# mLSTM and mixture-of-experts kernel: another searched order of work

## The chip, the cores and the metric

The kernel runs on one core of a Trainium2 chip. The metric is device time in microseconds; the kernel before takes 465.71 us as the median of three runs (465.06 to 465.93).

## The reference

An mLSTM attention layer over 4 sequences, 8 heads, 768 steps and head size 40, and behind it a feed-forward layer on all 3072 tokens, everything in float32:

```python
for t in range(S):
    m_new = np.maximum(f_gate[:, :, t] + m, i_gate[:, :, t])
    f_stab = np.exp(f_gate[:, :, t] + m - m_new)
    i_stab = np.exp(i_gate[:, :, t] - m_new)
    m = m_new
    C = f_stab[:, :, None, None] * C + i_stab[:, :, None, None] * np.einsum('bhd,bhe->bhde', vt, kt)
    n = f_stab[:, :, None] * n + i_stab[:, :, None] * kt
    h_tilde = np.einsum('bhde,bhe->bhd', C, qt)
    nq = np.einsum('bhd,bhd->bh', n, qt)[:, :, None]
    denom = np.maximum(np.abs(nq), 1.0)
    y[:, :, t] = o * h_tilde / denom
...
h = x @ w_in
relu6 = np.clip(h + 3.0, 0.0, 6.0)
g = h * relu6 / 6.0
return (g @ w_out).astype(np.float32)
```

Here vt, kt, qt are step t of v, k and q, o is the sigmoid of o_gate, and w_in and w_out (320 x 2048 and back) come as float64.

## The kernel before, in words

The recurrence is computed in chunks of 128 steps. A pair is one chunk of one sequence; there are 24 pairs, each in two groups of four heads ("quads"), which makes 48 chunk tasks. The tokens of the pairs are gathered into seven blocks, numbered 0 to 6, of 2, 2, 4, 4, 4, 4 and 4 pairs. A block first has its attention computed, then it is transposed (xa, line 613), split into a high and a low part for exact float32 products (xh on ACT, line 621, and xl on DVE, line 623), multiplied with w_in in 16 slices (mm1, line 738), passed through the activation (re on ACT, line 755, and gg on DVE, line 757), split again (gh, line 205 or 207, and gl, line 768), and multiplied with w_out in 8 steps per pair (mm2, lines 784 to 786). Block 0 has its second product in native float32 (line 781). Each pair's accumulator is copied out (ev) and stored.

The attention of a chunk task has loads (st, line 354, and nat, line 359), a weighing of the keys by the gates (vp, line 368 on ACT, line 370 on DVE or POOL), small matmuls in groups (xya and xyb, lines 479 to 512: S and K of a task, and B of the task before), the state C (line 452 or 455, its first form a copy on line 205 or 207), a gate window gw (a mask gm on line 401, a shift gc on line 406, an exponential gx on line 416, or on line 414 in four pieces with the shift in it), the products with it (fr, line 419), and the outputs (b1, b2, r1 to r3, o1 and o2, lines 464, 469 and 593 to 598). Four gate blocks (g0 to g3) are made by scans on DVE (lines 274 to 286); a transposition on PE (pT) and three copies (cTs, cT, gTs) lead to wT, the weights of vp.

The weights arrive as float64 in sixteen slices of 640 KB, eight of w_in (raw buffers called rawi) and eight of w_out (rawo). Three raw buffers are shared by all of them. Float64 is taken apart by hand: ACT reads a slice three times (w1, line 648; w2, line 653; w3, line 658), DVE puts it together (w4 to w6, lines 663, 664 and 669 or 674), and a slice of w_in is then split into whi, wlo and the two tail pieces th and ts (lines 205, 207, 692, 693 and 695), a slice of w_out later into vh and vl (lines 205 or 207, and 710).

Nothing of this is ordered by a loop at run time or by a scheduler. A table of 1,886 entries, the string ORDER, fixes it. Each entry is a number of an operation, a letter for the engine (p is PE, d is DVE, a is ACT, g is POOL, q is the SP queue, n means that it is left out because another operation has taken it in) and, behind it, the numbers of the buffers that it takes. Entries of the form F are filler matmuls (line 232), whose result nobody reads. The kernel walks through the table once and emits each operation on its engine's queue; each engine executes its queue in order, and waits where its inputs aren't there or its buffer isn't free. The part that does this:

```python
        for tok in ORDER.split():
            if tok[0] == "F":
                fill(int(tok[1:] or 1))
                continue
...
            i = next(k for k, ch in enumerate(tok) if ch.isalpha())
            key, engs, fn, after, get = T.ops[int(tok[:i])]
            e, slots = tok[i], tok[i + 1 :].split("/") if len(tok) > i + 1 else []
...
            fn(e)
            done.add(key)
```

The table itself was searched outside of the kernel.

Of the kernel before, what the change touches and what calls it, by code (L numbers as in the profile page):

```python
# [57 lines left out]
719p0 F 132q 145g F 767d0 133g 134n 146n 122n 123d 768d 120d 721p10 80q0 949a F 950d F F F 81a 948a 770d 951g F 113d1 114d 769d 135a 952q1 F 124d 771g
125d 772d1 773d 774d 777p0 775d 953a1 956d 776d 780p10 957d 783g 784p20 954a0 955a 157q1 778a0 779d 147a 958d 129q4 130d F F 996q2 781a 782d 997a0 F F
785a 786d 128q4 722p0 960a 158q 159g 939d 137d 138n 139d 160g 998a1 963q0 1000d 143q0 965a0 144d 136d 907n 1068p0 1071p1 1069a 1070d 1074p0 22q 23d  # L60
964a2 1001d 142q1 723p0 959a 1072a 967d 1073d 155q1 156g 1077p1 25d 968d 1003q1 999a 1002d 1117p0 966a 969d 1075a 1076d 1004a0 1078a 1080p0 26d 1007d
149d 150n 962g 1079d 1083p1 151d 148d 27d 961d 971a 1005a1 970a 973g 1116p0 1081a 1082d 1086p0 1084a 1085d 140d0 141d 972d 1006a 198q3 154q0 168q3
1010q2 1011a1 1014d 1008d 197q2 169q2 170g 724p0 152d 1087a 1088d 163d 161a 1089p1 1092p0 24g 29d 1012a0 1013a 1009d 1118p 162d 153d 1090a 1091d 171g
172g 787d2 985q0 986a2 31p31 164n 165d 725p0 1093a 1094d 989d 32d 36p 182q4 28q 974q1 987a1 988a 35a 33a 975a0 1015d 1016d 990d 991d 1095p0 976a0
1017q2 978d 993d 979d 34a 1018a1 1021d 37d 1096a 1097d 166d1 1120p 1022d 167d 977a 980d 38a 1119p 1098p1 1101p0 1019a1 1020a 1023d 1121p 173a 1099a
239q0 183q4 174d 39a 184g 191n 175d 1122p 176n 177d 788d 789d 1100d 981a 984g 726p0 982a 983d 185q2 1102a 1103d 1024q0 1025a1 1028d 992a 1104p1 1107p0
1029d 995g 178d 179d 792d0 1026a0 1027a 793d 126q0 1030d 1123p 1125p 127a 994d 1108a 1109d 1038q1 1110p0 1031q2 252q0 1033a1 30d 790d 240q 224q1 795d
1032a0 1035d 1036d 1105a 1034a 1111a 1040a0 791g 1106d 1112d 1124p 1037d 1052a 1113p1 1114a 797p0 798a1 794d 796d 1115d 803a 799d 186q 200g 201n 187d
1039a1 1127p 1053g 804p1 217g 40q 192d 193g 805a 806d 800p0 801a 226g 1126p 188n 802d 189a 190d 230n 194d 1045q0 1046a2 1136p1 1141p0 1137a0 199d
727p0 211q2 1138d 1146p1 223q1 1042d 1049d 1043d 1041a 1142a1 1143d 1044d 213d 1050d 1151p0 225d 1128p 1047a1 1048a 1051d 214n 1129p 1144a0 1145d  # L70
210q0 180q0 202a 241d 195d0 203d 1147a1 1148d 204g 205d 196d 251q3 41q 280g 1139a1 236q4 212g 1054d 1140g 253a 1130p 1132a0 242n 206n 207d 1152a0 42d
44d 43g 1153d 1131p 1134a1 237q4 1149a2 1150d 728p0 218d 1055d 1154a3 1155g 219n 220d 227n 228a 284n 308q3 281n 1156p1 1161p0 1216p0 1218p 1157a1
1158d 45d 46d 267d 208d 209d 1217p0 47q 215a 1162a0 1056a 1163d 1166p1 1171p0 49d 1159a0 1219p 1160g 1164d1 1165d 216d 729p0 282a 1057d 1167a1 1172a0
1168d 1176p1 1169d2 1170g 1173d 1181p0 231d 232n 1174d3 181a 1177a1 295q1 1220p 221d 222d 229d 1178d 271g 238g 245g 233d 730p0 246d 234d 235d 807d1
1058a 254g 51p31 247n 248d 277q2 243a 346q0 1175g 1059g 1060a 1061g 244d 296q 278q2 1182a0 297d 1183d 1062d 808d 809d 255g 1063g 52a 1222p 54a 53a 55a
279a 1221p 1179a0 1184a1 731p0 249d1 56p 265q1 266a 58a 57d 59a 268n 1180g 258n 259d 260n 1186p0 264q1 261d 256a 257d 250d 298n 1185d 50d 301g 1064a
1191p1 1192a1 1193d 1223p 732p0 1065d 262d 263d 1194a2 1195g 310g 355g 272d 1196p1 1224p 269a 270d 340n 273n 274d 733p0 1225p 1197a0 1198d 810d 1133q
1201p1 811g 1199a3 1200g 1187a1 285d 1188d 1206p0 292q4 293q4 275d 375q0 311n 312a 276d 283d 309a 286n 287d 294g 734p0 1202a0 1189d0 299a 1203d 1204d1
1190d 1205d 817p1 288d 1207a1 1208d 302d 289d 1066a 307q3 349q2 350q 323d 1226p 1228p 362q1 812d2 818a0 819d 813d 1211p0 1212a0 815d 814d 816d 823a
1067g 1227p 1209a0 1229p 333q1 374q2 334q2 1210g 824p1 1213d 1214a2 1215g 303n 304d 300d 735p0 305d0 313d 825a 826d 820p0 821a 822d 327n 324n 336d  # L80
306d 337n 1230p 314g 315d 316n 1232a2 364d 1231p 1234d0 1236p1 1241p0 1237a1 1238d 1239d1 321q4 322g 1246p1 1242a0 365d 1243d 1251p0 320q4 1244d3 317d
736p0 1240d 1252a1 1245d 1316p0 1247a0 1253d 318d 319d 376a 325a 328d 329g 335g 351g 352d 353a 1319p0 1317p0 1318p0 330d 1248d 394n 326d 1254a0 1255g
1256p0 1257a1 366a 1258d 338a 737p0 341d 342g 331d 1249d2 347q3 1261p1 1266p0 348d 343d 1250d 1323p 1320p 1322p 1259a1 1260d 332d 1267a0 418q4 1268d
390d 339d 738p0 354d 356d 357g 361q3 344d 345d 1271p0 1321p 1269a3 1262a1 1263d 1276p1 1270d 363d 358d 739p0 359d1 1264a0 1265g 1277a0 1327p 1272a1
1325p 1326p 1278d 1281p1 367d 1273d 1274a2 360d 1286p0 1324p 391d 392a 290q0 291a 1275g 1282a1 1283d 1330p 381g 1291p1 1284d0 1285d 368g 369d 370n
371d 740p0 478n 1287a1 1329p 1331p 388q2 389d 403q3 404a 827d0 1288d 48q 405q0 406q 407g 408n 1279a1 411g 372d 377d 382d 383n 1280d 1292a0 1334p 1293d
830d 384d 387q4 828d 61q 60q 62d 373d 829d 1233q 1296p0 1328p 1335p 378d 379a 63g 1294a2 1295d 1297a0 1332p 1289a3 1290g 1301p1 420g 1302a1 1333p
1298d 1299a0 380d 741p0 395d 1303d 393d 385d 1306p0 396n 386d 424g 1300g 1337p 1307a0 409a 397d 459q1 402q1 471q0 831g 1308d 431q1 432a 742p0 837p1
838a1 1304d1 417q3 1339p 1305g 1311p0 1312a1 412d 413n 398d 399d 832d1 833d 834d 835d 836g 1338p 1342p 1336p 1313d 1314a2 410d 414d 839d 840p0 1135q
460q 843g 487g 504g 419g 743p0 425d 426n 415d0 841a 842d 844p1 845a 400q0 1341p 1343p 846d 1356p0 1361p1 1309d3 1310g 1315d 1345p 491g 1357a0 1340p  # L90
1346p 64d 65d 66d 421d 416d 1347p 1358d 1359d0 68q 427d 1366p0 1352a2 1350d1 1360d 1344p 401a 1362a1 1363d 1371p1 1364d1 422a 423d 1365d 1367a0 1368d
69d 1369d2 1376p0 461d 1372a1 1373d 1370d 485q0 465g 446g 1381p1 447g 1351q 457q2 456q2 444q3 67q 1235q 445a 1437p0 430q4 744p0 569q2 472q4 437g 438d
1354d1 1374a3 1348a0 1438p0 433g 1436p0 1439p0 1353q 570q 607q1 434n 435a 436d 1375d 439n 440d 1442p 1377a0 1378d 458a 428d 429d 1440p 448a 462n
# [828 lines left out]
```

## Time and profile before

| | |
|---|---|
| median of 3 runs | 465.71 us (465.06 to 465.93) |
| the profiled execution | 464.87 us |
| its span, first to last instruction | 463.2 us |
| granted TensorE clock, mean | 0.996 |
| PE busy | 449.1 us (97%) |
| DVE busy | 298.8 us (65%) |
| ACT busy | 215.8 us (47%) |
| POOL busy | 122.4 us (26%) |
| chain that ended last | PE 85%, DVE 9%, ACT 2%, issue 1%, DMA 1% |

The busy shares are means over the whole span. They differ by stage, so the stages are read one by one from the windows. A matmul's duration includes its way through the array, and consecutive ones overlap; the distance of two starts is what one adds.

### The profile page before, as it was taken

The page shows a single profiled execution, that of the slowest core. Times are in us where ns is not written, and L with a number is a line of the kernel's source. Part 1 is how long each engine was busy: PE and PEld are TensorE (multiplying, and loading weights), DVE is VectorE, ACT ScalarE, POOL GpSimd, SP SyncE. Part 2 cuts the span into 40 slices and gives each one's busy share as a digit, 9 for nine tenths or more (in the row PEclk, how much of TensorE's full clock was granted, in tenths as well). Part 3 has the DMA queues.
Part 4 walks back from the last instruction along what each step waited for, and adds up shares of the span by engine and source line. Part 5 has one row for each costly group of instructions (what it writes and reads, how often), then busy time and mean ns, then how long its engine had stood idle before and what let it go on. Part 6 is the DMA issues. An engine that isn't in the chain of part 4 may idle for free.

```text
span 463.2 us, 12600 instructions
## 1 busy us (share of the span) xinstructions
PE 449.1 (97%) x5243; PEld 388.3 (84%) x5249; DVE 298.8 (65%) x752; ACT 215.8 (47%) x482; POOL 122.4 (26%) x155
## 2 busy tenths in 40 slices
PE   8879989999999999999999999999999999999997
PEld 4547767899888888988889988988989898989896
DVE  6999999978866376856655763576555646443423
ACT  5788798777343434263343353243551232321231
POOL 3152225265311307502213134132112201020130
PEclk9989999999999999999999999999999999999999
DMA  6998887276304450244421442432322000010001
GB/s 208 281 315 265 234 258 203 59 176 169 94 20 119 119 151 4 78 142 121 115 77 44 131 139 60 108 102 89 101 69 78 1 1 1 16 57 1 1 1 57
DMA packets 24977, 49.38 MB, mean 107 GB/s; under 512 B 2840, under 2 KB 15960, under 8 KB 24920
## 3 DMA queue, kind: packets, MB, share of 16 engines
q1 hardware_dynamic: 24696, 47.89, 35.5%
...
q10 hardware_dynamic: 224, 0.69, 0.5%
...
## 4 chain that ended last, share of the span: by engine, by line
PE 85%; DVE 9%; ACT 2%; issue 1%; DMA 1%; SPq 0%; DVEq 0%; ACTq 0%
PE h L738 35%; PE acc L784 11%; PE acc L785 11%; PE acc L786 11%; PE xya L506 3%; PE xya L479 3%; PE pw L232 2%; PE xya L489 2%; PE xa L613 2%; PE xya L512 2%; PE acc L781 1%; DVE on L597 1%; DMA st<-in_qk_dram 1%; DVE on L598 1%; DVE gv L757 1%
## 5 line engine op out<-in xcount | busy, mean ns | idle before, releaser
L755 ACT ACTIVATE g<-h,half 128x512 f32<-128x512 f32 (+1 forms) x96 | 61.8, 651 | 128.3 <-PE h L738 92.9
L784 PE MATMUL acc<-vh,gh 128*128 128x320 f32 x352 | 111.5, 317 | 0.0
L757 DVE SCALAR_TENSOR_TENSOR g<-g,h 128x512 f32<-128x512 f32 (+1 forms) x96 | 61.2, 640 | 77.4 <-ACT g L755 77.3
L785 PE MATMUL acc<-vl,gh 128*128 128x320 f32 x352 | 108.6, 309 | 0.0
L786 PE MATMUL acc<-vh,gl 128*128 128x320 f32 x352 | 108.5, 308 | 0.0
L768 POOL TENSOR_TENSOR gl<-g,gh 128x512 fp32r<-128x512 f32 (+1 forms) x40 | 48.7, 1222 | 183.6 <-DVE gh L207 104.2
L738 PE MATMUL h<-xh,whi 128*128 128x512 f32 (+1 forms) x224 | 83.9, 375 | 2.4 <-DVE gv L757 1.7
L738 PE MATMUL h<-xh,wlo 128*128 128x512 f32 (+1 forms) x224 | 80.8, 361 | 0.0
L738 PE MATMUL h<-xl,whi 128*128 128x512 f32 (+1 forms) x224 | 80.5, 360 | 0.0
L784 PEld LDWEIGHTS acc<-vh,gh 128*128 128x128 f32 x352 | 66.0, 188 | 2.5
L785 PEld LDWEIGHTS acc<-vl,gh 128*128 128x128 f32 x352 | 66.1, 188 | 1.8
L786 PEld LDWEIGHTS acc<-vh,gl 128*128 128x128 f32 x352 | 66.0, 188 | 0.0
L738 PEld LDWEIGHTS h<-xh,whi 128*128 128x128 f32 x224 | 42.0, 187 | 11.4 <-DVE gv L757 3.7
L205 ACT CAST gh<-g 128x512 fp32r<-128x512 f32 (+1 forms) x53 | 30.0, 571 | 39.8 <-PE acc L785 19.5
L738 PEld LDWEIGHTS h<-xh,wlo 128*128 128x128 f32 x224 | 42.1, 188 | 6.9
L768 DVE TENSOR_TENSOR gl<-g,gh 128x512 fp32r<-128x512 f32 (+1 forms) x56 | 40.0, 722 | 12.2 <-ACT gh L205 10.9
L738 PEld LDWEIGHTS h<-xl,whi 128*128 128x128 f32 x224 | 42.1, 188 | 4.5
L738 PE MATMUL h<-xl,wtl 128*128 128x512 f32 (+1 forms) x112 | 40.5, 361 | 0.0
L738 PE MATMUL h<-xh,wtl 128*128 128x512 f32 (+1 forms) x112 | 40.2, 359 | 0.0
L419 DVE TENSOR_TENSOR gw<-xya,gw 128x256 f32<-128x256 f32 x48 | 20.0, 416 | 10.7 <-PE xya L489 7.4
L452 DVE SCALAR_TENSOR_TENSOR C<-C,dec,xya 128x42 f32<-128x42 f32 x100 | 20.6, 251 | 9.1 <-PE xya L489 9.0
L207 DVE CAST gh<-g 128x512 fp32r<-128x512 f32 (+1 forms) x43 | 19.3, 451 | 7.5 <-PE acc L785 6.1
(136 smaller groups left out, 683.2 us busy)
## 6 DMA issues: line engine op xcount, KB each, us to landing
...
rawo<-in_w_out_dram SPq DMA_DIRECT2D x8, 640.0 KB, 7.9
...
rawi<-in_w_in_dram SPq DMA_DIRECT2D x7, 640.0 KB, 8.5
...
on<-in_on_dram SPq DMA_DIRECT2D x5, 640.0 KB, 4.9
rawi<-in_w_in_dram ACTq DMA_DIRECT2D x1, 640.0 KB, 4.2
```

The source lines that it names most:

```text
L205: nc.scalar.copy(dst, src)
L207: E(c).tensor_copy(dst, src)
L419: add(f"fr{nm}", "d", lambda e: nc.vector.tensor_tensor(V["gw", task][:, cp], V["xy", "S", nm][:, :, 0:128].rearrange("p c (j t) -> p j c ...
L452: nc.vector.scalar_tensor_tensor(Cn[:, j], cur[:, j], dc[:, j : j + 1], kv[:, hc, j], ALU.mult, ALU.add)
L479: nc.tensor.matmul(xy[h * Q : h * Q + Q, c, j * Q : j * Q + Q], st[rs, j, h], st[rs, j, 2 + (h != c)], start=True, stop=True)
L738: nc.tensor.matmul(hp[:, :n], w, x[:, :n], start=k == 0, stop=k == len(seq) - 1)
L755: nc.scalar.activation(V["g", nm], V["h", nm][:, :n], AF.Relu, bias=half, scale=1.0 / 6.0)
L757: add(f"gg{nm}", "d", lambda e: nc.vector.scalar_tensor_tensor(V["g", nm], V["g", nm], 1.0, V["h", nm][:, :n], ALU.min, ALU.mult), [f"re{n ...
L768: add(f"gl{nm}", "gd", lambda e: E(e).tensor_sub(V["gl", nm], V["g", nm], V["gh", nm].bitcast(F32)), [f"gh{nm}"], kind="tt", n=n, lock=1)
L784: nc.tensor.matmul(acc, gh[:, ts_], V["VH", f // 4][:, f % 4, :], start=f == 0, stop=False)
L785: nc.tensor.matmul(acc, gh[:, ts_], V["VL", p][:, f % 2, :], start=False, stop=False)
L786: nc.tensor.matmul(acc, gl[:, ts_], V["VH", f // 4][:, f % 4, :], start=False, stop=f == NF - 1)
```

## The change

Only the table ORDER is another. The operations, their code and their dependences stay. It came out of the same search with another measure: the end of an order is judged as its mean over draws of random delays on loads and operations, in place of its end without delays. The new table has 1,883 entries, 46 F for 49. It also gives some operations to other engines: DVE has 658 entries for 685, ACT 369 for 365, POOL 163 for 143. Every line of the table differs; the first of them:

```diff
--- before.py
+++ after.py
@@ -51,78 +51,78 @@
 ORDER = """
-1a 908a0 T F F F F 2q 3d 4d 5d F F F F F 6d 7d 9d F 909a0 912d 913d F F 910a0 107p0/0 F 0q 16d 11p0 12d 919q1 911a 914d 916d 917d 14a F F 920a1 923d
...
+1a 908a0 T F F F 2q 3d F F 0q 16d 5d 6d F F F F 4d 7d 910a0 9d 85p0/0 11p0 F F 96p10 F F 909a0 911a 86a 919q1 920a1 941q2 921a1 922a 82q0 912d 913d
...
```

Three places show how it moves instructions. The first is ACT from its third pass over weight slice 0 on. In the names a number follows each buffer; rawi_128 is slice 0, the next ones in both lists are slice 1, cTs and wT are the gate weights, gw the gate window. Before, cTs stands directly behind slice 0:

```order
7 L658 ACTIVATE lwi_155<-rawi_128,tiny 128x640
8 L205 COPY cTs<-pc_169 128x32
9 L648 ACTIVATE yi_188<-rawi_177 128x640
10 L653 ACTIVATE lwi_191<-rawi_177 128x640
11 L388 ACTIVATE gw_0_194<-gb_0_0_195 128x256
12 L319 ACTIVATE dec<-pc_169 128x32
13 L321 ACTIVATE wT<-wT 128x32
```

And with the change (rawi_226 is slice 2, rawi_188 slice 3):

```order
7 L658 ACTIVATE lwi_149<-rawi_128,tiny 128x640
8 L388 ACTIVATE gw_0_152<-gb_0_0_153 128x256
9 L648 ACTIVATE yi_186<-rawi_184 128x640
10 L653 ACTIVATE lwi_190<-rawi_184 128x640
11 L658 ACTIVATE lwi_190<-rawi_184,tiny 128x640
12 L653 ACTIVATE lwi_228<-rawi_188 128x640
13 L306 ACTIVATE eG<-pc_161 128x32
14 L648 ACTIVATE yi_232<-rawi_226 128x640
15 L648 ACTIVATE yi_235<-rawi_188 128x640
16 L205 COPY cTs<-pc_161 128x32
```

The copy cTs has moved behind all of slice 1 and the first reads of slices 2 and 3.

The second place is the SP queue, which issues the loads, from its first weight slice on; st and nat are the data of chunk tasks, gsc a small scratch store that waits for the first gate scan. Before:

```order
3 L640 DMA rawi_177<-in_w_in_dram 128x1280
4 L285 DMA gsc<-f_s 4x8x128
5 L359 DMA nat_0_1_216<-in_nat_dram 128x412
6 L354 DMA st_0_0_218<-in_qk_dram 112x640
7 L359 DMA nat_0_0_220<-in_nat_dram 128x412
```

With the change:

```order
3 L640 DMA rawi_184<-in_w_in_dram 128x1280
4 L640 DMA rawi_188<-in_w_in_dram 128x1280
5 L354 DMA st_0_0_193<-in_qk_dram 112x640
6 L285 DMA gsc<-f_s 4x8x128
7 L640 DMA rawi_226<-in_w_in_dram 128x1280
8 L359 DMA nat_1_1_244<-in_nat_dram 128x412
9 L359 DMA nat_0_0_247<-in_nat_dram 128x412
```

Slice 3 is now issued right behind slice 1, and slice 2, whose buffer was slice 0's, ahead of the chunk loads.

The third place is PE around the first mm1 matmul of block 0 (h_0). Before, it follows the group xya4 (here xya_559, with S and K of one task):

```order
155 L479 MATMUL xya_559<-st_0_0_557 64x64 x8
156 L489 MATMUL xya_559<-nat_0_0_542 64x42 x8
157 L738 MATMUL h_0_610<-xh_533,whi 128x256
158 L738 MATMUL h_0_610<-xl_534,whi 128x256
```

With the change, the group xya5 (here xya_614) ends directly ahead of it, while xya4 stands ahead of the transposes:

```order
155 L506 MATMUL xya_614<-C_0_0_0_588,st_0_0_557 64x42 x4
156 L512 MATMUL xya_614<-nat_0_0_533,gw_0_345 64x42 x8
157 L479 MATMUL xya_614<-st_0_1_388 64x64 x8
158 L489 MATMUL xya_614<-nat_0_1_531 64x42 x8
159 L738 MATMUL h_0_677<-xh_598,whi 128x256
```

One group more precedes the first mm1.

## Rows read from the trace of the kernel before

**Rows 1.** Windows: length, then busy us of PE, PEld, DVE, ACT, POOL; clock, DMA.

```profile
0.00:34.62 34.62, 29.00 (x385) 16.67 (x392) 28.31 (x83) 24.39 (x53) 12.00 (x23) 0.95 0.86 268
34.62:76.34 41.72, 37.98 (x443) 30.08 (x435) 39.90 (x101) 34.86 (x66) 13.74 (x16) 1.00 0.82 241
...
sum 463.20, PE 449.12 PEld 388.31 DVE 298.84 ACT 215.75 POOL 122.44; mean PE 149.71 PEld 129.44 DVE 99.61 ACT 71.92 POOL 40.81
```

**Rows 2.** Groups of instructions by form: busy us, mean ns, idle before and releaser.

```profile
L232 PE MATMUL pw<-ones 128*128 128x512 bf16 x43 | 14.9, 475 | 3.1 <-issue 1.8 <-DVE tiny L179 1.3
```

**Rows 3.** The window from ACT's first weight slice to its third xh.

```profile
5.59:33.13 27.54, 23.18 (x343) 14.47 (x348) 23.69 (x67) 21.44 (x48) 7.44 (x10) 0.96 0.92 281
```

**Rows 4.** PE's waits from 76.34 on: for whom, us, times, longest.

```profile
PE xa L613 <- ACT on L205: 0.8, 1, 0.8
PE xa L613 <- DVE g L757: 0.6, 1, 0.6
```

**Rows 5.** ACT's groups by form, from 5.59 to 33.13.

```profile
L658 ACT ACTIVATE lwi<-rawi,tiny 128x640 f16<-128x640 f32 x5 | 5.0, 998 | 0.0
L653 ACT ACTIVATE lwi<-rawi 128x640 uint16<-128x640 uint32 x5 | 4.5, 909 | 0.0
L648 ACT ACTIVATE yi<-rawi 128x640 f32<-128x640 f32 x5 | 4.0, 792 | 2.1 <-DMA rawi<-in_w_in_dram 2.1
...
L388 ACT ACTIVATE gw<-gb 128x256 f32<-128x256 f32 x4 | 1.5, 382 | 0.8 <-PE gb L384 0.8
L205 ACT CAST whi<-yi 128x512 fp32r<-128x512 f32 x2 | 1.2, 595 | 0.0
...
L205 ACT COPY C<-xya 128x84 f32<-128x84 f32 x2 | 0.5, 229 | 2.3 <-DVE gw L419 2.2
```

**Rows 6.** ACT's groups by form, whole span.

```profile
L414 ACT ACTIVATE gw<-gw,cT 128x64 f32<-128x64 f32 x88 | 23.3, 338 | 0.0
...
L368 ACT ACTIVATE nat<-nat,wT 128x40 f32<-128x40 f32 x60 | 14.7, 318 | 11.1 <-DMA nat<-in_nat_dram 11.1
```

**Rows 7.** Timeline of ACT, its third pass over slice 0: start, us.

```profile
7.05 1.00 ACT L658 ACTIVATE lwi<-rawi,tiny 128x640 f16<-128x640 f32 x1
```

**Rows 8.** Loads of w_in slices: the one from ACT's queue, then SP's seven.

```profile
rawi<-in_w_in_dram ACTq DMA_DIRECT2D x1, 640.0 KB, 4.2
...
DMA to landing us min/median/max: 6.5/8.5/10.6
```

**Rows 9.** Timeline of PE: the first matmuls of the first two mm1.

```profile
34.62 0.38 PE L738 MATMUL h<-xh,whi 128*128 128x256 f32 x1
...
35.67 0.28 PE L738 MATMUL h<-xh,whi 128*128 128x256 f32 x1
```

**Rows 10.** Timeline of PE: one xya group to the next, a native second product.

```profile
114.46 0.44 PE L506 MATMUL xya<-C,st 40*64 40x42 f32 x16
...
115.54 0.66 PE L613 MATMUL xa<-ident,on 128*128 128x128 f32 x4
...
75.48 1.24 PE L781 MATMUL acc<-vr,gv 128*128 128x320 f32 x4
```

**Rows 11.** DVE's groups by form, whole span.

```profile
L674 DVE CUSTOM_DVE_ANT_0 yi<-yi,lwi 128x1280 uint16<-128x1280 uint16 x8 | 6.7, 843 | 0.3
...
L692 DVE TENSOR_TENSOR wtl<-yi,wtl 64x128 fp32r<-64x128 f32 x8 | 3.4, 425 | 0.3
...
L693 DVE TENSOR_TENSOR wtl<-yi,wtl 64x128 fp32r<-64x128 f32 x8 | 2.3, 288 | 0.2
```

**Rows 12.** Timeline of DVE: a sum of gate block 1.

```profile
38.28 0.99 DVE L276 TENSOR_TENSOR f_s<-f_s,m_s 64x128 f32<-64x128 f32 x1
```

**Rows 13.** Timeline of POOL and DVE near 117 us, and of DVE near 75.

```profile
116.61 1.57 POOL L710 TENSOR_TENSOR vl<-vr,vh 128x640 fp32r<-128x640 f32 x1 [2.77 <-ACT vh L205]
...
116.68 1.78 DVE L401 TENSOR_TENSOR gw<-gw,mask 128x256 f32<-128x256 f32 x1
...
75.07 0.41 DVE L401 TENSOR_TENSOR gw<-gw,mask 128x256 f32<-128x256 f32 x1
```

More of the change, by code (lines that the diff above doesn't have):

```diff
@@ L58 @@
[L58 to L93, printed above, removed]
@@ new lines @@
+721p0 109d 768d 110a 111n 112d 719p10 955a 958d 81a F F F F 770d 113d1 143q1 146n 129q2 130a 134g 144g F 965a1 147a 769d F 157q0 28q 124d 125d 772d1
+128q0 722p0 771g 777p0 114d 773d 774d 135a 959a 775d 776d 783g 137a F F 960a 780p10 F 781a0 778a 784p20 136d F 1002d F F 138n 139d 723p0 962g 779d
+785a 786d 782d 966a 974q1 975a1 976a0 967d 968d 969d 185q1 154q2 155q0 907n 1068p0 149d 1069a 1070d 158q 169q3 159g 140d0 978d 971a 972g 1071p1 1072a
+1074p0 1073d 1077p1 150n 151d 148d 141d 156a 724p0 197q1 961d 970a 1075a 1076d 1078a 1079d 1080p0 1083p1 160g 29d 977a 985q0 986a2 1003q2 1005a1
@@ new lines @@
+1257a1 333q4 330d 737p0 331d 332d 337n 1319p0 340n 341d 342n 343d 338a 1262a0 1263d 339d 1234a0 1317p0 1322p 1264a0 1266p0 1323p 1258d 1271p1 1259a1
+362q1 361q3 347q3 348g 738p0 354d 1321p 363g 1265g 1267a0 1268d 1260g 368g 1326p 1276p0 1269a2 344d 356d 345d 357g 358d 739p0 1270g 1272a1 1273d
+1281p1 374q2 405q2 406q 407d 375q2 403q0 369d 411g 1274a3 1275g 364d 365n 387q4 60q 366a 379a 370n 371d 376d 444q4 450n 437n 359d1 360d 367d 1325p
+388q3 740p0 382d 1330p 1324p 1327p 1277a0 1328p 420d 446g 389d 372d 373d 383g 384d 1282a1 1283d 1286p1 1284d0 421g 1285d 1287a1 380d 1288d 50d 741p0
@@ new lines @@
+1340p 1344p 425d 839d 1356p0 500g 501n 426g 1361p1 1345p 415d0 65d 66d 427d 1343p 67q 1357a0 1358d 1366p0 445d 434n 1362a1 1363d 63d 1350a2 1348d0
+458d 1364d0 69d 1365g 1367a1 1359a1 435a 1371p1 423d 472q0 416d 744p0 438d 436d 471q0 1368d 1351q 1346p 1352a2 428d 1360g 1372a0 1347p 515q1 1437p0
+516q 1349q 1353q 443q3 439n 1369a2 1370g 1133q 1373d 1374d3 429d 1376p0 1436p0 491g 1381p1 440d 745p0 635q1 400q0 1375d 1354a0 1355q 1382a1 1383d
+1440p 441d 1439p0 1438p0 451d 448a 442d 465n 452g 1377a0 1378d 1379d0 453d 1380d 449d 68q 528q3 1386p1 71p30 502a 1384a1 517g 1385g 746p0 487g 1387a0
@@ new lines @@
+1577p 651a 875d 876d 883d 688n 878a1 681q2 1551p1 633d0 634d 641d 1545g 1552a0 1553d 879d 1554a0 1555d 1581p 1549a2 1550g 1580p 760p0 654d 652d 880p1
+881a 884p0 885a 1582p 706g 1586p 1583p 882d 1592a0 644d 886d 1596p1 1597a0 1598d 1599d1 1600g 1601p0 1602a1 1587p 1585p 1606p1 1607a0 1603d 1611p0
+692q1 1594a1 1595q 659g 645d 761p0 663d 655d 704q3 1608d 1584p 665d 1604a3 1605g 1678p0 1612a1 1679p0 669q0 670g 1613d 1614a0 1615g 1609d2 1610d
+1616p1 1621p0 1590a1 1593q 656d 762p0 666d 1588a0 675a 1676p0 1680p 667d 887d1 888d 1617a1 1618d 1677p0 693q4 694a 1622a0 1683p 1626p1 1681p 620q0
@@ new lines @@
+676d 705g 1623d 1624d1 1625d 1619d3 678d 696d 697a 1591q 1627a0 1628d 1471q 1682p 1620g 1631p0 1632a1 889d 1633d 1684p 763p0 679d1 1629a0 1636p1
+1641p0 1686p 1687p 1685p 1634d2 685n 686a 687d 1635g 1589q 1637a1 1638d 1630d 680d 689d 764p0 690d 1688p 1642a0 1639a1 1646p1 621a 1640g 1647a1 1691p
+707n 1643d 691d 700d 1651p0 1689p 1644d3 1645d 1690p 1652a0 1694p 698d 1648d 1649a0 1656p1 1653d 1654d2 703q0 765p0 70d 701d 708a 709d 1655g 711d
+1661p0 702d 766p0 712d 1650d 713d 1657a0 1658d 892d0 1693p 1695p 1692p 1662a1 1699p 1666p1 895d 1663d 1671p0 1696p 1659a1 1660d 890d 891d 1667a0
@@ L126 @@
+1750d 1810p 1762a0 1763d 1766p0 1811p 1808p 1758d 1771p1 1759a1 1764a3 1765g 1760g 1814p 1809p 1772a0 1767a1 1773d 1774a0 1815p 1768d 1776p1 1781p0
+1769a2 1775d 1770g 1813p 1812p 1818p 1777a0 1782a1 1783d 1786p0 1778d 1784d1 1817p 1785g 1787a1 1791p1 1788d 1816p 1819p 1779d3 1780g 1822p 1792a0
+1793d 1794d0 1823p 1789a2 1820p 1790d 1795d 1827p 1834a2 1835q 1824p 1821p 1826p 1825p 1828d0 1829q 1832a1 1833q 1830a2 1831q
 """
```

83 lines of the change are left out of this document (48 added, 35 removed).

## The prediction

> **What bounds the kernel now.** I read the busy times first. The matrix engine (PE) is busy 449.12 of 463.20 us [rows 1], and the change leaves every matmul that computes something as it is, so only PE's other time can change. That is the idle time, 14.1 us, and the filler matmuls on line 232, 14.9 us [rows 2]; together 29.0 us, 20.5 of it before the first mm1 matmul.
>
> Next the windows, cut where the first mm1 of token block 0 starts (34.62 us) and where that of block 1 starts (76.34 us) [rows 1]. Up to 34.62, PE is busy 29.00 us, of which 14.9 are fillers. From there to 76.34, PE idles 41.72 - 37.98 = 3.74 us beside a vector engine (DVE) that is busy 39.90 of 41.72. After 76.34, PE idles what is left of the 14.1, 4.7 us. The list of waits has 0.8 and 0.6 of that, both ahead of transposes (xa) [rows 4]; the rest is the output tail behind the last matmul. So the time is decided in three places: the start, where DVE and ACT prepare block 0 and the first weight slices; the middle, bound by DVE; and the block boundaries later.
>
> **Term A, the start.** The operations stay the same; the table hands some to other engines and puts all in another order. Ahead of the third xh copy, the order shows ACT 10 operations longer. By kind and mean [rows 5, 6]: one more absolute value of a slice (0.79), two more L653 (0.91 each), one more L658 (1.00), three weighings (L368, four instructions each, 14.7 / 15 = 0.98), one more whi cast (0.60), three C copies (0.23), one small copy less (0.2, like C's), and one gate exponential in one piece instead of four (0.38, as L388, for 23.3 / 22 = 1.06). Sum 0.79 + 1.82 + 1.00 + 2.94 + 0.60 + 0.69 - 0.2 - 0.68 = 7.0; back-to-back ACT instructions overlap by about a tenth (the first three last 0.79 + 0.91 + 1.00 = 2.70 and take 2.46, from 5.59 to 7.05 + 1.00 = 8.05 [rows 7]), so 6.3.
>
> Before, ACT was busy 21.44 us from 5.59 to 33.13, idle 6.1 [rows 3]. The new list takes 27.7, so without any idle its last xh ends at 33.3, as before. How much it idles is the question. One wait is plain in the order: the copy cTs, on which wT, the weighings and so the whole block hang, now stands behind the absolute value of slices 2 and 3, and ACT takes its queue in order. Slice 2 is loaded into slice 0's buffer, so SP cannot issue it before ACT's third pass over slice 0 ends at 8.05. Landing: 4.2 us for the one slice that ACT's own queue issued, 6.5 / 8.5 / 10.6 as least, median and most of those from SP [rows 8]. ACT has work ahead of it until 5.59 + 0.9 x (0.91 + 0.79 + 1.00 + 0.38 + 0.79 + 0.91 + 1.00 + 0.91 + 0.23) = 11.8, the operations ahead of it in its new order. I take 6.5, since little is in flight so early: landed 14.5, idle 2.7. For other waits I take 0.8, what ACT waited for the gate matmuls before [rows 5]. So the last xh ends at 33.3 + 3.5 = 36.8, and the first mm1 follows 1.49 later, as before (33.13 to 34.62 [rows 3, 9]): 38.3, 3.7 later. One group (xya5), 1.08 us (114.46 to 115.54 [rows 10]), now stands ahead of it and no longer behind. **A = +2.6**, with ends -0.9 (no idle) and +6.8 (landing in 10.6); with the median landing +4.7.
>
> Two moves ahead of the first mm1 I price at nothing. Three fillers are gone; they only filled PE's waits, and the first mm1 waits for xl. The st load of the third task that runs is SP's 22nd instruction instead of its 16th, behind slice 4, which waits for slice 2's buffer. By the same rows ACT's third pass over slice 2 ends 0.9 x 6.4 behind 14.5, at 20.3, and with the 4.2 of an early load the data lands near 25; its C copy on ACT stands 17 operations later, near 29, which hides it. If that load takes 8.5, the cover is gone.
>
> **Term B, the middle.** Between the last xl of block 0 and the last xl of block 1, DVE's list falls from 92 operations to 80. By the rows [rows 11, 12], three ts pairs less (0.43 + 0.29 each, 2.1; two of them go to POOL), two L674 less (1.7) and the L276 of gate block 1 less (0.99, now in the start) are 4.8 us, 4.3 with a tenth off for overlap. The other six of the twelve, one kind against another, I price at the stretch's mean, 39.90 / 92 = 0.43 each, 2.6. Together 6.9. DVE's busy time falls to 33.0; with its idle 1.82 and 0.7 for the closer coupling to ACT, which has 55 operations here for 64, the stretch takes 35.5. But one mm1 of block 0 (1.05, 34.62 to 35.67 [rows 9]) and three native second products (1.24 each [rows 10]) have moved behind its end, 4.77 us still to be paid. **B** = 35.5 - 41.72 + 4.77 = **-1.5**. Ends: PE's own work, 37.98 - 4.77 = 33.2, cannot be undercut, -3.7; with PE idling 3.74 as before, 0.
>
> **Term C, after it.** At block 2, PE has one second product (six matmuls) less between the last group of the block and the first transpose behind it that waits for all of it; at block 6 it has three more. So the 0.8 may grow, and the 0.6 goes. The 0.8 has a visible cause: the mask addition L401 on DVE took 1.78 instead of 0.41, beside a POOL vl of 1.57 that began 0.07 earlier [rows 13]; in the new table that vl is issued elsewhere. The output tail keeps its form. **C = 0**, ends -1.5 (both waits gone) and +1.5.
>
> POOL gets 20 operations more, 12 of them gl. I price them at nothing: POOL is busy 122.44 of 463.20 us [rows 1]. That cover goes if POOL holds DVE up where DVE ends a wait, as it did in that row. The Trainium skill, SBUF — State Buffer, section "Who interferes with whom", states that a DVE instruction with two SBUF inputs contends with a GpSimd instruction that reads SBUF, and that whoever issues first keeps the pair for its whole length. The trace agrees at this place (1.78 beside 1.57). By the row alone the moved gl cost nothing; by the rule each can hold up DVE, which is rival 3.
>
> **Sum.** A + B + C = 2.6 - 1.5 + 0 = +1.1. The profiled execution took 464.87 us (span 463.2); it would become 466.0. The median of the runs is 465.71, 0.84 above it, so the forecast is 465.71 + 1.1 = **466.8 us**. About 0.2%, 0.93 us, is what a measurement of this kernel can tell from no change.
>
> **Rivals.**
> 1. Faster. The slice lands in 4.2 us like the first one: at 12.25, idle 0.45 + 0.8, first mm1 at 36.0, A = +0.35; DVE and ACT do not hold each other up, B = -2.2 (without the 0.7); the wait at block 6 goes, C = -0.6. Sum -2.4, **463.3**. For it: early on there is less in flight, and DVE is lighter by 12 operations. Against it: no slice from SP landed in under 6.5. It decides from a first mm1 before 37.2. Chance 0.28.
> 2. No change. The wait is 2.4 in all, the first mm1 comes at 37.2, A = +1.5, and B gives it back exactly: **465.7**. For it: the middle absorbs whatever DVE had ready. This is also the case of the change not doing what it says: another order of the same work with the same total. Chance 0.24.
> 3. Much slower. A and B as forecast, but POOL's new gl hold up DVE in three of the five later block boundaries, 1.37 each (1.78 - 0.41), less the 0.84 that is paid already: +3.3, **470.1**. Against it: DVE is busy only 230.63 of 386.86 us there (298.84 less 28.31 and 39.90 [rows 1]). Chance 0.08.
>
> **The numbers.** The forecast, slower by about 1.1 us, has 0.40; its own range is 465.5 to 468.5. Slower by over 0.2% gets it and rival 3, 0.48; no change 0.24; faster 0.28. The range for all, 463.6 to 469.8, reaches down nearly to rival 1 (its worse half lies inside) and up to A with the median landing and a little of C; the far ends of A and B together are left out.
>
> **What would show it.** In the new profile: ACT idle until about 14.5 us behind a weight-slice load; the first h matmul near 38.3 (rival 2: 37.2, rival 1: under 37); DVE busy about 33 us between there and the start of block 1, and that stretch near 35.5; PE idle after it still about 4.7, with the wait at block 6 gone. I am wrong if the first mm1 starts by 36, if the middle takes 38 or more, or if PE idles over 7 us after the start of block 1.

## The result, and the profile after

The changed kernel takes 471.12 us (median of 4 runs, 470.38 to 473.25) where the kernel before takes 465.82: a ratio of 1.0119, 95% interval 1.0092 to 1.0147. It is slower, and it lies above the range that was given. Run again later it took 472.78 us (6 runs, 471.40 to 474.47), 1.0129 (1.0091 to 1.0167). The first profiled execution, 470.38 us, is the fastest of all ten. Medians are over all executions of a kernel, while a ratio and its interval leave out the few in a slower state.

First the busy times of the page, and the granted clock of PE in 40 slices:

```profile
PE 453.6 (97%) x5246; PEld 391.8 (84%) x5246; DVE 286.4 (61%) x726; ACT 218.9 (47%) x486; POOL 144.0 (31%) x177
...
PEclk9599999899999999999999999999999999999999
```

DVE has less to do and POOL more, as the table says [rows 1]. PE is busy longer with three fillers less and otherwise the same matmuls: some of them ran at half the clock, in the second slice and the eighth.

The windows, cut at the same events as before (ACT's first slice to its third xh; the first mm1 of block 0; that of block 1), with the columns of [rows 1]:

```profile
6.23:37.26 31.03, 28.70 (x375) 16.82 (x374) 26.00 (x73) 27.19 (x63) 7.47 (x11) 0.78 0.94 295
0.00:39.69 39.69, 34.48 (x446) 19.77 (x446) 32.30 (x94) 31.10 (x68) 11.56 (x24) 0.83 0.89 276
39.69:73.73 34.04, 32.19 (x426) 27.18 (x421) 31.76 (x90) 30.78 (x69) 13.84 (x19) 1.00 0.84 240
73.73:468.70 394.97, 386.96 (x4382) 344.88 (x4380) 222.34 (x545) 157.03 (x351) 118.61 (x135) 1.00 0.26 77
```

The span grew by 468.7 - 463.2 = 5.5 us. In the prediction's terms: **A**, the first mm1 at 39.69 for 34.62, less the group of 1.08 now ahead of it, +4.0; **B**, 34.04 - 41.72 + 4.77 = -2.9; **C**, the rest, 5.5 - 4.0 + 2.9 = +4.4. The forecast had +2.6, -1.5 and 0. Of C, 3.3 is idle time of PE (8.0 for 4.7), and the other 1.1 is work of PE that took longer.

PE's waits behind 73.73, to be set against [rows 4]:

```profile
PE h L738 <- DVE gv L757: 2.8, 1, 2.8
PE xya L506 <- DVE ht L469: 1.5, 1, 1.5
PE xa L613 <- DVE on L598: 0.3, 1, 0.3
```

The waits of 0.8 and 0.6 are gone; 2.8 and 1.5 have come. The timeline of all engines around the longer one (start, length, engine, line, tiles):

```profile
84.91 0.50 POOL L370 TENSOR_TENSOR nat<-nat,wT 128x160 f32<-128x160 f32 x1
85.01 2.75 DVE L279 TENSOR_TENSOR f_s<-f_s,m_s 64x256 f32<-64x256 f32 x1
...
85.37 0.61 POOL L406 TENSOR_TENSOR gw<-gw,cT 128x256 f32<-128x256 f32 x1
...
85.95 1.53 POOL L710 TENSOR_TENSOR vl<-vr,vh 128x640 fp32r<-128x640 f32 x1
...
88.72 0.41 DVE L757 SCALAR_TENSOR_TENSOR gv<-gv,h 128x256 f32<-128x256 f32 x1
...
89.18 0.39 PE L738 MATMUL h<-xh,whi 128*128 128x256 f32 x1 [2.80 <-DVE gv L757]
...
90.50 3.70 PE L781 MATMUL acc<-vr,gv 128*128 128x320 f32 x8
```

L279 is a gate sum that takes 0.41 us in the kernel before. Here it lasts through three POOL instructions. The gv behind it on DVE frees the buffer that PE's next mm1 waits for, so PE stands for 2.80 us. Then the clock falls (0.66 from 89.18 to 94.20), and eight native second products take 3.70 us for 2.3.

The start differs from profile to profile. First DVE in the first profile; then, from the second one of the same kernel, DVE and PE on the timeline, and PE's clock in a window (columns as above):

```profile
4.20 0.24 DVE L316 COPY last<-ident 128x128 f32<-128x128 f32 x1
5.16 0.41 DVE L283 TENSOR_TENSOR_SCAN f_s<-one,f_s 64x128 f32<-64x128 f32 x1
```

```profile
5.82 0.23 DVE L316 COPY last<-ident 128x128 f32<-128x128 f32 x1 [1.31 <-DMA ident<-in_ident_dram]
6.70 0.41 DVE L283 TENSOR_TENSOR_SCAN f_s<-one,f_s 64x128 f32<-64x128 f32 x1
...
7.16 1.22 PE L381 MATMUL gb<-f_s,sel 64*128 64x128 f32 x4 [1.67 <-DVE f_s L283]
...
11.44 1.22 PE L381 MATMUL gb<-f_s,sel 64*128 64x128 f32 x4
12.59 1.12 PE L384 MATMUL gb<-sel,i_s 64*64 64x128 f32 x8
...
42.41 0.39 PE L738 MATMUL h<-xh,whi 128*128 128x256 f32 x1
```

```profile
10.00:15.00 5.00, 5.00 (x28) 3.08 (x28) 3.76 (x9) 2.99 (x4) 0.00 (x0) 1.00 0.92 311
```

The copy `last` (L316) stands ahead of the gate sums in the new table, and waits for the constants' load. In the first profile that load had landed; in the second it had not, and the first mm1 came 2.7 us later. But the two profiles differ in one thing more: L381 and L384 take 1.22 and 1.12 us from the first gate block on in the second, and 0.71 and 0.66 in the first two gate blocks of the first. The kernel "gc, vl, and cT" below has the same start, as its edits lie behind 80 us, and its profile has the slow matmuls almost without the late constants. DVE, PE and ACT in it, then the same operation of ACT in the first profile:

```profile
4.49 0.23 DVE L316 COPY last<-ident 128x128 f32<-128x128 f32 x1 [0.99 <-DMA ident<-in_ident_dram]
...
5.83 1.22 PE L381 MATMUL gb<-f_s,sel 64*128 64x128 f32 x4 [0.34 <-DVE f_s L283]
...
14.21 0.20 ACT L306 ACTIVATE eG<-pc 128x32 f32<-128x32 f32 x1 [2.38 <-PE pc L314]
...
41.51 0.39 PE L738 MATMUL h<-xh,whi 128*128 128x256 f32 x1
```

```profile
12.73 0.20 ACT L306 ACTIVATE eG<-pc 128x32 f32<-128x32 f32 x1 [0.70 <-PE pc L314]
```

The gate scan is only 0.2 us later than in the first profile (5.37 for 5.16), but ACT waits 2.38 us for PE's small matmuls, eG comes 1.5 us later and the first mm1 1.8. So the 2.7 us of the second profile can't be put down to the constants alone.

Profiles of the start of the kernel before have the first mm1 at 34.62, 34.66 and 36.96 (the last is that of the kernel with two POOL entries on DVE, below, whose edits begin at 117 us), so that start varies too.

### The profile page after: what moved, and what is told of

Same layout as the page of the kernel before. It is cut to its first block, busy times and chain, and to the rows that moved or that the text cites. A ratio compares the mean times of both kernels' runs of the same rounds, so it can differ in the third digit from the quotient of the medians.

```text
span 468.7 us, 12607 instructions
## 1 busy us (share of the span) xinstructions
PE 453.6 (97%) x5246; PEld 391.8 (84%) x5246; DVE 286.4 (61%) x726; ACT 218.9 (47%) x486; POOL 144.0 (31%) x177
## 4 chain that ended last, share of the span: by engine, by line
PE 80%; DVE 11%; ACT 5%; DMA 2%; issue 1%; ACTq 0%; DVEq 0%
PE h L738 35%; PE acc L784 12%; PE acc L785 11%; PE acc L786 11%; PE xya L506 3%; DMA rawi<-in_w_in_dram 2%; PE xya L479 2%; PE xya L512 2%; PE acc L781 2%; PE xa L613 2%; PE xya L489 2%; DVE gv L757 1%; DVE yi L674 1%; DVE vr L669 1%; DVE yi L664 1%
## 5 line engine op out<-in xcount | busy, mean ns | idle before, releaser
L768 POOL TENSOR_TENSOR gl<-g,gh 128x512 fp32r<-128x512 f32 (+1 forms) x52 | 64.7, 1250 | 175.8 <-DVE gh L207 79.3
L738 PE MATMUL h<-xh,whi 128*128 128x512 f32 (+1 forms) x224 | 85.0, 379 | 4.2 <-DVE gv L757 3.7
L205 ACT CAST gh<-g 128x512 fp32r<-128x512 f32 (+1 forms) x57 | 33.1, 589 | 53.9 <-DVE g L757 40.9
L768 DVE TENSOR_TENSOR gl<-g,gh 128x512 fp32r<-128x512 f32 (+1 forms) x44 | 28.7, 660 | 7.3 <-ACT gh L205 6.5
L464 DVE TENSOR_TENSOR ht<-xya,eG 128x168 f32<-128x168 f32 x43 | 14.0, 326 | 23.5 <-PE xya L489 23.5
L443 POOL TENSOR_TENSOR C<-C,dec 128x84 f32<-128x84 f32 x27 | 11.0, 408 | 54.9 <-DVE C L452 25.0
```

Source lines behind the costliest of these rows:

```text
L205: nc.scalar.copy(dst, src)
L443: nc.gpsimd.tensor_tensor(Cn, cur, dec[:, c, hc, k : k + 2][:, :, None].broadcast_to([128, 2, E2]), ALU.mult)
L464: nc.vector.tensor_tensor(hv, V["xy", "B", nm][:, :, 212:296].rearrange("p h (j e) -> p h j e", j=2), heads(eG[:, c], quad, b)[:, :, :, No ...
L738: nc.tensor.matmul(hp[:, :n], w, x[:, :n], start=k == 0, stop=k == len(seq) - 1)
L768: add(f"gl{nm}", "gd", lambda e: E(e).tensor_sub(V["gl", nm], V["g", nm], V["gh", nm].bitcast(F32)), [f"gh{nm}"], kind="tt", n=n, lock=1)
```

## The experiments

| kernel | median us | ratio to before, 95% interval | first mm1 |
|---|---|---|---|
| changed, again | 472.78 | 1.0129 (1.0091 to 1.0167) | 42.41 |
| gc and vl to DVE | 468.17 | 1.0038 (1.0020 to 1.0056) | 42.31 |
| 8 fillers at L310 | 471.92 (without the one of 2443) | 1.0136 (1.0098 to 1.0174) | - |
| wli to DVE | 471.24 | 1.0102 (1.0069 to 1.0135) | 40.52 |
| cTs early | 471.97 | 1.0118 (1.0086 to 1.0150) | 42.18 |
| constants' copy back | 470.07 | 1.0083 (1.0055 to 1.0110) | 39.25 |
| 5 fillers at the first gb | 470.82 | 1.0095 (1.0063 to 1.0127) | 41.80 |
| gc, vl, and cT | 468.00 | 1.0046 (1.0018 to 1.0074) | 41.51 |
| four edits | 465.85 | 0.9990 (0.9966 to 1.0015) | 38.97 |
| four edits, gates first | 468.50 | 1.0056 (1.0029 to 1.0084) | 40.47 |
| four edits, 5 fillers | 466.34 | 1.0005 (0.9980 to 1.0029) | 40.44 |
| four edits, shorter lists (1) | 474.96 | 1.0154 (1.0124 to 1.0184) | 42.95 |
| four edits, shorter lists (2) | 466.67 | 1.0027 (1.0003 to 1.0052) | 38.52 |
| before, constants' copy early | 468.67 | 1.0070 (1.0035 to 1.0104) | 37.43 |
| before, two POOL entries to DVE | 464.60 | 0.9957 (0.9938 to 0.9976) | 36.96 |

All are edits of the table alone. In the diffs a line is one entry; a moved entry stands between its new neighbours.

**POOL's hold at 85 us.** The shift gc and the vl go from POOL to DVE, each at its place in the table:

```diff
-242g
+242d
...
-1057g
+1057d
```

> The changed kernel with two entries given from POOL to DVE: the shift gc (L406) and the vl (L710) that POOL ran while DVE's gate sum L279 took 2.75 us at 85.01. Theory 1 (POOL kept DVE out, and PE's wait of 2.8 us, the half clock from 90 to 93.5 us and the 1.5 us wait near 103 us all follow from that one instruction): L279 under 0.9 us, PE's wait at 86.4 under 1 us, clock 1.0 near 90, the wait near 103 under 0.5; 4 to 6 us less than the changed kernel's 471.1, so 465 to 467. Theory 2 (only the instruction's own lateness counts, the clock and the later wait have causes of their own): L279 short, but 1.5 to 2.8 us less, 468.3 to 469.6. Theory 3 (L279 was long for a reason of its own): L279 stays over 2 us and the time at 471.

Timeline of DVE, then PE:

```profile
87.24 0.94 DVE L279 TENSOR_TENSOR f_s<-f_s,m_s 64x256 f32<-64x256 f32 x1
...
89.74 0.39 PE L738 MATMUL h<-xh,whi 128*128 128x256 f32 x1 [0.55 <-DVE gv L757]
90.79 2.32 PE L781 MATMUL acc<-vr,gv 128*128 128x320 f32 x8
```

L279 falls from 2.75 (2.74 to 2.75 in six profiles with those entries on POOL) to 0.94, the wait from 2.80 to 0.55, and the eight products run at full speed. The wait of 1.5 near 103 stayed, at 1.4. The median is 3 to 4.6 us below the changed kernel's two. Both entries were new on POOL: the kernel before has 1057d and 242n (its shift was part of the exponential). So POOL's hold is the cause of the 2.8 us. Theory 1 is right on that; it missed the later wait and the time, 468.17 us for 465 to 467.

The half speed does not follow from the wait alone. In six profiles with L279 at 2.74 or 2.75 and the wait at 2.80, the eight products took 3.25 to 4.42 us four times and 2.31 twice, here with the constants' copy back (PE):

```profile
88.62 0.39 PE L738 MATMUL h<-xh,whi 128*128 128x256 f32 x1 [2.80 <-DVE gv L757]
...
89.67 2.31 PE L781 MATMUL acc<-vr,gv 128*128 128x320 f32 x8
```

**That later wait.** On top of the first experiment, cT goes ahead of the tanh on ACT:

```diff
-181a 53a
+53a 181a
```

> The first experiment (gc and vl from POOL to DVE) and one swap on ACT besides: the copy cT of gate block 2 ahead of the tanh of an o-gate block (L340, 1.28 us) instead of behind it. PE still waited 1.4 us near 102 us there, for ht, and DVE's wT waited 0.6 us for cT. Theory (the chain cT, wT, C, ht sets that wait, and the tanh stands in it): the wait falls to 0.3 us or less, 1.0 to 1.4 us less than the first experiment's 468.2, so 466.8 to 467.2. Rival (DVE's own queue ahead of ht sets it; wT waited only 0.6): 0.6 us less or nothing.

PE's wait for ht (view of waits):

```profile
PE xya L506 <- DVE ht L469: 0.7, 1, 0.7
```

Half of the wait went, the rest did not; the time cannot be told from the first experiment's. The rival had it. What sets the other half was not tried.

**The constants' copy.** Moved back behind the first two weight operations (912d, 913d); and, the other way, load and copy moved to the front in the kernel before:

```diff
-16d 5d
+5d
...
 912d 913d
+16d
```

```diff
+0q 16d
 5d
...
-0q 16d
```

> The changed kernel with one entry moved: the copy of the constants (L316, last) on DVE stands behind the first two weight operations of slice 0, as in the kernel before, and no longer ahead of the gate sums. Theory of the late constant: DVE's gate scan L283 is done by 5.7 us in every profile, PE's wait for it is 0.5 us or less, the first mm1 at 39 to 40 us even if the ident load lands late; 1 to 2 us less than the changed kernel beside it. Rival (the lists of ACT and DVE set the start, whatever the first microseconds do): no difference in time beyond 0.5 us.

> The kernel before with one entry moved the other way: the constants' load and copy (L316) ahead of the gate sums on DVE, as in the changed kernel. Theory of the late constant: DVE waits 1 to 2 us at L316, the gate scan ends near 7 instead of 5.6 us, the first mm1 comes 1 to 2.5 us later than 34.6, and the time is 0.7 to 2.5 us more than the kernel before. Rival (the kernel before has 12 fillers and slack there): within 0.5 us of it.

The changed kernel with the copy back, then the kernel before with it in front (DVE, PE):

```profile
5.29 0.41 DVE L283 TENSOR_TENSOR_SCAN f_s<-one,f_s 64x128 f32<-64x128 f32 x1
...
39.25 0.39 PE L738 MATMUL h<-xh,whi 128*128 128x256 f32 x1
```

```profile
5.84 0.23 DVE L316 COPY last<-ident 128x128 f32<-128x128 f32 x1 [1.25 <-DMA ident<-in_ident_dram]
6.62 0.42 DVE L283 TENSOR_TENSOR_SCAN f_s<-one,f_s 64x128 f32<-64x128 f32 x1
...
37.43 0.35 PE L738 MATMUL h<-xh,whi 128*128 128x256 f32 x1 [0.43 <-DVE xl L623]
```

In the kernel before the early copy costs 2.7 us (468.67 for 465.95), 1.0070 with an interval clear of 1; there L381 and L384 keep their 0.71 and 0.66, so it is not the slow matmuls. In the changed kernel the copy back gains 1.0 to 2.7 us (470.07 for 471.12 and 472.78, with overlapping intervals), which is not shown clear of noise. The times carry this more than the two first mm1s do: since the start of the kernel before has 36.96 in one profile without the edit, part of 37.43 may be the draw of the loads.

> The changed kernel once more, for a second profile and its time on the same chip as the kernels beside it. In the first profile the constants' load (ident) landed before DVE came to its copy (L316, last), which stands ahead of the gate sums in the changed order; in three experiments with the same start it landed later, DVE waited 1.3 to 1.8 us and the first mm1 came up to 2.6 us later. Theory of the late constant: again a wait of DVE at L316 of over 1 us, PE waiting 1.6 us for the gate scan, gate-block matmuls (L384) of 1.12 instead of 0.66 us from about 10 us on, first mm1 at 41.5 to 42.5. Rival (the first profile is the typical one): first mm1 at 39.7.

> The kernel before once more, for a second profile of its start. If the start of the kernel before depends on the first loads as that of the changed kernel does, its first mm1 lies more than 1 us from 34.62; if not, within 0.7 us.

These two second profiles stand in the first section: the changed kernel's has the numbers of its theory, in which late constants and slow matmuls come together, and that of the kernel before (465.11 us, first mm1 34.66) repeats the first.

**POOL's hold at 36 us.** wli goes to DVE behind the three xl:

```diff
-962g
 779d 785a 786d 782d
+962d
```

> The changed kernel with one whi-side split (wli, L695), which POOL ran at 36.08 for 1.28 us beside DVE's L669 of 1.86 us, given to DVE behind the three xl of block 0. Theory 1 (POOL kept DVE out there too, and the three xl and the first mm1 waited behind it): L669 back to 0.8 us, the first mm1 about 1.0 us earlier, at 38.7; in the end 0.3 to 1.0 us less than 471.1, as DVE takes 0.7 us more in the middle. Rival (the xl wait for xh and xa anyway): the first mm1 stays at 39.7 and the time is the same or 0.7 longer.

DVE beside POOL in the changed kernel, and DVE with the edit:

```profile
36.08 1.28 POOL L695 TENSOR_TENSOR wlo<-yi,whi 128x512 fp32r<-128x512 f32 x1
...
36.18 1.86 DVE L669 CUSTOM_DVE_ANT_0 vr<-yo,lwo 128x1280 uint16<-128x1280 uint16 x1
...
38.31 1.07 DVE L623 TENSOR_TENSOR xl<-xa,xh 128x256 fp32r<-128x256 f32 x3
```

```profile
38.06 0.82 DVE L669 CUSTOM_DVE_ANT_0 vr<-yo,lwo 128x1280 uint16<-128x1280 uint16 x1
```

The hold went, and from the end of ACT's third xh to the first mm1 it is 1.39 us (39.13 to 40.52) for 2.43. In this run the constants came late (scan at 6.67); against the second profile of the changed kernel (scan at 6.70, first mm1 at 42.41) the first mm1 is 1.9 us earlier. The time alone does not tell it.

**cTs early.** 14a moves ahead of 931a2, the first read of slice 2:

> The changed kernel with the copy cTs on ACT moved ahead of the first reads of slices 2 and 3. The prediction's theory (cTs stands behind a slice that must land, and the whole block hangs on it): cTs 1.7 us earlier than 14.59, the first mm1 1 to 2 us earlier, time 469 to 470. Rival (ACT waited for that slice only 0.3 us, and the start is set by the length of ACT's and DVE's lists): the first mm1 within 0.4 us of 39.69, time 471.

The copy came at 14.74 us, no earlier than the 14.59 of the first profile, because eG ahead of it waited 2.44 us for PE's pc. Against the second profile, which like this one has late constants (scan at 6.89 here, 6.70 there) and cTs at 16.96, it is 2.2 us earlier; the first mm1 is only 0.2 us earlier (42.18 for 42.41), and the time did not move. The prediction's cause for ACT's idle time falls.

**PE's half speed in the start.** Three ways to keep PE busy: 8 fillers ahead of L310, 5 ahead of the first gate block, and 5 ahead of L310 in the kernel with four edits.

> The changed kernel with 8 more filler matmuls on PE ahead of its first small matmuls behind gTs (L310), where PE idled 1.6 us up to 11.51 and the granted clock then stood at 0.5 until about 25 us. Theory of the clock (the slow PE makes the gate-block matmuls late, with them SP's loads queued behind them, and with these the fifth weight slice, for which ACT waited 1.1 us at 27.59): the clock stays at 1.0 from 10 to 25 us, slice 4 is issued up to 1.9 us earlier than 22.29, and the first mm1 comes 1 to 1.5 us earlier than 39.69; time 469.6 to 470.1. Rival (ACT and DVE's own lists set the start, PE has slack there at either clock): the first mm1 stays within 0.4 us of 39.69, time 471.

> The changed kernel with 5 more filler matmuls ahead of the first gate-block matmul, where PE otherwise idles for the gate scan. Theory of the clock (what the start loses is PE at half clock from about 10 to 25 us, and that comes from PE's idle times before 12 us): L384 takes 0.66 us in all four gate blocks, the third xya is 1 to 2 us earlier and so is the first mm1; 1 to 2 us less than the changed kernel. Rival (half clock is only where PE has slack): first mm1 not earlier than the changed kernel's beside it, time the same or up to 1 us longer, as the fillers stand ahead of the gate blocks.

> The kernel with four edits, and 5 more filler matmuls ahead of L310 on PE, where it idled 1.1 us and the gate-block matmuls then took 1.12 instead of 0.66 us until about 20 us. Theory (the half speed makes the third and fourth gate block late, with them the loads behind them): L384 0.66 us in the third gate block at least, first mm1 0.7 to 1.5 us earlier than 39.0, and the time 0.5 to 1.5 us less. Rival (the start hangs on ACT's and DVE's lists): first mm1 within 0.4 us of 39.0 and the same time.

The first of them cost time or did nothing (five executions from 471.2 to 475.4; a sixth, the profiled one, took 2443 us, and its trace isn't read). With 5 at the first gate block L384 took 0.66 in three blocks of four, and the first mm1 came 0.6 us earlier than 42.41. The third, in its profile (PE):

```profile
13.91 0.66 PE L384 MATMUL gb<-sel,i_s 64*64 64x128 f32 x8
...
40.44 0.39 PE L738 MATMUL h<-xh,whi 128*128 128x256 f32 x1
```

Full speed through the gate blocks, where the kernel with four edits has 1.12, no earlier first mm1 and no time gained (466.34 for 465.85). This does not show that the start is free of PE's speed: in this profile the first weight slice landed later (ACT's first read at 6.68 us for 5.64), and the profile in the first section, with its wait of 2.38 us for PE, speaks against it. It shows that the fillers are no gain.

**All four edits.** 

> The changed kernel with all four edits: the constants' copy behind the first weight operations, wli from POOL to DVE behind the three xl, gc and vl from POOL to DVE at 85 us, cT ahead of the tanh. Theory (the losses are separate and add up: about 2.7 at the constants, 0.7 to 1 at wli, 3.9 at gc and vl, 1.2 at cT, from 472): 463 to 465, faster than the kernel before by 1 to 3 us, first mm1 at 38 to 39, PE waiting under 2 us in all from 76 us on. Rival (they overlap, so that one's gain is the other's slack): 466 or more.

PE's waits from 73.2 us on:

```profile
PE h L738 <- DVE gv L757: 0.7, 1, 0.7
PE xya L506 <- DVE ht L469: 0.7, 1, 0.7
PE xa L613 <- DVE on L598: 0.3, 1, 0.3
PE xya L506 <- DVE C L452: 0.2, 1, 0.2
```

465.85 us, the kernel before within the interval: the four edits give back the whole loss of 5.3 to 6.7 us, though not the 1 to 3 us more that the theory had.

**What is left of the start.** The first mm1 still comes near 39, not at 34.6. Three tries: the gates ahead of the weights (12d ahead of 912d, 15a 14a 18d 20a ahead of 943a0, the first weighing as 84d, the nat loads ahead of 930q0); 965a1 and 999a behind xh and 1002d behind xl; the same without 999a.

> The kernel with all four edits, and in the start the gates ahead of the weights besides, as in the kernel before: gTs ahead of slice 0's weight operations on DVE, eG, cTs and wT ahead of the third read of slice 1 on ACT, the first weighing on DVE, and the four nat loads ahead of slice 2's load on SP. Theory (what is left of the start's loss, 39.2 against 34.6 us, is chunk work queued behind weight slices): first mm1 1 to 3 us earlier than in the kernel with four edits, and the time 0.5 to 2 us less. Rival (the weight operations must all be done before the first mm1 anyway, the order among them does not matter): first mm1 within 0.5 us, no gain.

> The kernel with four edits, and three weight operations that the first mm1 doesn't need moved behind xh and xl: on ACT the third read of w_out slice 0 (L658, 1.03 us) and the second read of w_in slice 5 (L653, 0.91), on DVE the combination of w_out slice 0 (L669, 0.82). Theory (the start is the length of ACT's and DVE's lists ahead of the first mm1): ACT's last xh and the first mm1 1.5 to 2.5 us earlier than 39.0, about 37; DVE has them to do in the middle, which gives back a part, so the time is 0.3 to 1.5 us less than with four edits, 464.4 to 465.5. Rival (loads or the chain through PE set the start): first mm1 within 0.5 us of 39.0.

> The kernel with four edits, and two weight operations that the first mm1 doesn't need and that free no load's buffer moved behind xh and xl: on ACT the second read of w_in slice 5 (L653, 0.91 us), on DVE the combination of w_out slice 0 (L669, 0.82). Theory (the start is the length of ACT's and DVE's lists ahead of the first mm1): xh and the first mm1 0.8 to 1.7 us earlier than 39.0 or than the second draw of it (40.4), so 37.3 to 39.6; the time 0 to 1.2 us less than with four edits. Rival (loads or the chain through PE set the start): first mm1 within 0.4 us, at 39 to 40.4, and the same time.

The first made it later, 40.47, with a new wait of 2.1 for a state C. The second was a mistake that teaches something; SP's waits and issues in it:

```profile
SPq L640 <- ACT lwo L658: 13.0, 1, 13.0
```

```profile
29.96 0.43 SPq L354 DMA_DIRECT2D st<-in_qk_dram  x1
43.49 0.33 SPq L640 DMA_DIRECT2D rawi<-in_w_in_dram  x1
```

The moved read (999a) frees the raw buffer of the next slice load, and SP, which issues in order, held every load behind it for 13 us. The third got 0.45 us earlier (38.52), ACT then idle 0.75 us for the transposes, and no time. So neither the order of gates and weights nor ACT's list alone sets these 4 us, and more speed of PE did not give them back; what does stays open. The profile of the four edits has one candidate that no run moves by itself: the load of a w_in slice, issued at 21.55, on which ACT waits 2.1 us up to 27.86, and from there the chain that ended last runs along ACT and DVE to the third xh.

**POOL's hold in the kernel before.** The vl of [rows 13] and one gl near 388 us go to DVE:

```diff
-1067g
+1067d
...
-1660g
+1660d
```

> The kernel before with two entries given from POOL to DVE: the vl that stood beside the mask addition of 1.78 us at 116.7, and the gl that stood beside L597 of 1.92 us at 388.1. Theory (POOL's hold on DVE is paid where DVE ends a wait of PE, in any table): L401 and L597 back to 0.4 and 0.8 us, PE's waits of 0.84 us at block 2 and 0.61 us at block 6 gone; 1.0 to 1.5 us less than the kernel before, 464.5 to 465. Rival (the waits have another cause, or DVE's added 0.8 and 0.7 us take their place): the same time within 0.4 us.

The second of these places in the kernel before (POOL, DVE):

```profile
387.75 1.58 POOL L768 TENSOR_TENSOR gl<-g,gh 128x512 fp32r<-128x512 f32 x1 [23.37 <-DVE gh L207]
388.09 1.92 DVE L597 SCALAR_TENSOR_TENSOR on<-on,ht 128x640 f32<-128x640 f32 x1
```

With the edit, DVE, and PE's waits from 79.4 us on:

```profile
119.54 0.42 DVE L401 TENSOR_TENSOR gw<-gw,mask 128x256 f32<-128x256 f32 x1
...
390.20 0.82 DVE L597 SCALAR_TENSOR_TENSOR on<-on,ht 128x640 f32<-128x640 f32 x1
```

```profile
PE xya L506 <- DVE gw L419: 0.3, 1, 0.3
```

Both waits of [rows 4] are gone, 464.60 us for 465.97, 0.9957 (0.9938 to 0.9976): faster than both kernels, by two letters of the table. The profiled execution is the slowest of the 12 (466.18 us): its first mm1 came at 36.96, after PE had waited 2.67 us for DVE's wlo, and the edits lie behind that.

## Why the prediction was wrong, point by point

**Term C failed, by the step "I price them at nothing"** (POOL's 20 operations more). It measured +4.4 for 0, three times its end. POOL was idle enough; that was no cover, as the prediction's own sentence on the cover said. Rival 3 named the mechanism and came near the time (470.1), with a chance of 0.08. It had the wrong place and the wrong operations: not gl at the block boundaries, but a weighing, a gc and a vl in a row, in the middle of block 1. Its price of 1.37 is that of one POOL instruction; three in a row cost 2.34 (2.75 - 0.41). The eight products behind it took 1.4 longer (3.70 - 2.32), at half the clock, which other profiles with the same wait do not have. The other new wait, 1.5 for ht, goes by half when cT is moved on ACT; the other half is open. The two waits of [rows 4] did go, as C's lower end had it. "PE idles over 7 us after the start of block 1", given as what would show it wrong, came true: 394.97 - 386.96 = 8.0.

**Term A had the right sum for ACT and missed two things.** ACT was forecast busy 27.7 and idle 3.5, its last xh ending at 36.8; it was busy 27.19, idle 3.84, and ended at 37.26. That the idle time came out is luck, for its cause was not the one given: SP's slice loads landed in 4.0 to 6.0 us, cTs hardly waited (0.28 ahead of it), and moving it gave nothing. ACT's longest waits were 1.11 for a later slice, 0.70 for PE's pc and 0.66 for DVE. From the last xh to the first mm1 the step "follows 1.49 later, as before" failed: it took 2.43, as L669 was held by POOL ahead of xl. And the copy `last` was in the order and wasn't priced; nothing of it shows in the trace before, where it stands behind the gates. With it late, and with PE's slow matmuls from the first gate block on, A is 42.41 - 34.62 - 1.08 = +6.7, at the far end that the range left out.

**Term B had the right cause and half the size.** DVE was busy 31.76 in the stretch (33.0 forecast), the stretch took 34.04 (35.5). -2.9 for -1.5, and -3.0 in the second profile. DVE's busy time fell by 8.1 for 6.9, and its idle time rose by 0.46 for the 0.7 allowed. Of the six operations priced at the mean of 0.43, one was an L598 of 1.61. The two L674 were two L669, the same operation on slices of w_out and of nearly the same length (0.82).

So A and B sum to +1.1 both in the forecast and in the first profile. That is luck: A was 1.4 more and B 1.4 less than forecast, and in the second profile they sum to +3.7. The change lost its time in C, by POOL's hold above all, and in the start, where late constants and PE's slow matmuls both appear and the runs do not part them.
